# Six small stores from ScalarE in the middle of a decode kernel, and x's load ahead of b1's

## The chip, the core and the metric

The kernel runs on one core of a Trainium2 chip. The core has TensorE (PE in the profile; PEld is its weight load), VectorE (DVE), ScalarE (ACT), GpSimd (POOL) and SyncE (SP), which run side by side and wait for each other by semaphores, and 16 DMA engines that move data between HBM and the on-chip memory. SP and ScalarE each issue DMAs on a queue of their own (q1 and q10 in the profile). The metric is the device time of one execution in microseconds; less is better.

## The reference

One token x of width 1024 goes through a layer norm; the result feeds an attention branch over a cached window and an MLP branch with a layer norm of its own; both are added.

```python
def _A_ref(x, k_cache, v_cache, wq, wo):      # Hq = 32 heads, Hkv = 4, Dh = 128
    W = 4096                                   # the last 4096 of 65536 cached positions
    q = (x @ wq)                               # 1024 -> 32 x 128
    k = jnp.repeat(k_cache[:, :, Sk - W:, :], rep, axis=1)
    v = jnp.repeat(v_cache[:, :, Sk - W:, :], rep, axis=1)
    p = _softmax(scores(q, k) * (Dh ** -0.5))
    return (p @ v).reshape(B, Sq, Hq * Dh) @ wo

def _B_ref(x, w1, b1, w2, b2):                 # F = 3584
    y = _layernorm(x, axis=-1)
    h = _gelu(jnp.einsum("bsd,df->bsf", y, w1) + b1)
    return jnp.einsum("bsf,fd->bsd", h, w2) + b2

xn = _layernorm(A_x, axis=-1)
return A_x + _A_ref(xn, ...) + _B_ref(xn, ...)
```

All inputs and the output are bf16; the output is one row of 1024. The weights and the window of the cache are 39.9 MB, each byte used once.

## The kernel before

The kernel is written out by hand, engine by engine; each engine runs its instructions in the order in which they stand in the code, and `Track` objects count semaphores so that one engine can wait for another's instruction.

*Loads.* SP issues the large loads on one queue, in this order: w1 (L208), K in two halves (L199), wq in two halves (L191, 4 of 8 rows each); then, when PE has finished h (L367), w2 into the place of w1 and V in two halves; then, when PE has finished q (L481), wo in four chunks of 20, 8, 3 and 1 columns (L191) into the place of wq. Each such DMA has one contiguous row for each of 128 partitions: 56 KB for w1 and w2, 32 KB for half of wq, 16 KB for half of K or V, 40 KB for wo's first chunk. ScalarE issues three small loads at the very start: b1's row (L204, 16 pieces of 448 bytes), x's row (L205, 2 KB, one partition) and b2's row (L206).

*Compute.* PE turns x's row into a column (L289), and PE, DVE, POOL and ScalarE do the two layer norms (L292 to L316). PE adds b1 into the PSUM (L350 on; it waits for b1 there) and multiplies by w1 in a loop (h). POOL meanwhile makes constants: identity matrices, masks, zeroed tiles (LB among them, L248). DVE transposes K in eight pieces (turn_k, L326). ScalarE copies h's rows out (L373, L374), PE transposes them, DVE and ScalarE compute the GELU: its exponential is L406 on ScalarE, the only work of ScalarE between L374 and L425. PE multiplies by wq as its halves land (q, paced by SP through `s_row`, L370). After q, ScalarE and DVE copy q's rows (L425, L427); PE transposes them, DVE and ScalarE spread them into LB (L450, L451); PE computes scores against K (L334), DVE their maxima (L480), ScalarE the exponentials (L506), DVE transposes the probabilities (L510). PE then multiplies the MLP's hidden row by w2 (looped by `steps`), the probabilities by V (loop pv, after waiting for both halves of V), and DVE normalizes (L541 to L557). After some extra matmuls that keep PE's clock up (turn_over, L534), PE multiplies by wo as its chunks land: the first two are announced by SP (L562), the last two are waited for by PE. b2 and x are added on PE. ScalarE copies the result to ORow (L579) and stores it as four pieces of 512 bytes from four partitions (L581); SP waits for that store (L582).

L334 is the line of the helper `tile`, by which nearly all of PE's matmuls are issued; L326 is that of `turn_k`, L191 of `load_rows`, L199 of `load_cache`.

Of the kernel before, what the change touches and what calls it, by code (L numbers as in the profile page):

```python
# [10 lines left out]
D = 1024  # L11
# [39 lines left out]
def bass_parallel_sum__sliding_block_cached__mixer_channel_mlp__decode_kernel(  # L51
# [18 lines left out]
    pe, dve, act, pool, sp = nc.tensor, nc.vector, nc.scalar, nc.gpsimd, nc.sync  # L70

    def sems(name, n):
        return [nc.alloc_semaphore(f"{name}{i}") for i in range(n)]

    s_xrow, s_b1, s_b2, s_w1, s_w2, s_out, s_go, s_row = (
        nc.alloc_semaphore(n) for n in ("s_xrow", "s_b1", "s_b2", "s_w1", "s_w2", "s_out", "s_go", "s_row"))
    s_wq = sems("s_wq", len(WQ_CHUNKS))
    s_k = sems("s_k", NPAIR)
    s_v = sems("s_v", NPAIR)
# [5 lines left out]
    POOL = Track(nc, "S_POOL")  # L85

    def sb(name, shape, d):
        return nc.alloc_sbuf_tensor(name, shape, d)
# [14 lines left out]
    XBR = sb("XBR", [1, 2 * D], bf16)  # L103
# [9 lines left out]
    ORow = sb("ORow", [128, 256], bf16)  # L113
    QT = sb("QT", [128, HQ], bf16)
    LB = sb("LB", [128, 8 * 144], bf16)
# [27 lines left out]
    x_row = A_x.rearrange("b s n -> (b s) n")  # L143
# [6 lines left out]
    out_rows = out.rearrange("b s (a n) -> (b s a) n", a=4)  # L150

    C = {}
# [44 lines left out]
    def load_cache(dst, cache, semaphores):  # L197
        for i in range(NPAIR):
# [2 lines left out]
                cache[0, 2 * i:2 * i + 2, SK - W:SK, :].rearrange("g (m b) d -> m g (b d)", m=64),  # L201
            ).then_inc(semaphores[i], 16)

    act.dma_start(B1R, b1_row.rearrange("o (c n) -> o c n", c=B1N)).then_inc(s_b1, 16)  # L204
    act.dma_start(XBR[:, 0:D], x_row).then_inc(s_xrow, 16)  # L205
    act.dma_start(XBR[:, D:2 * D], b2_row).then_inc(s_b2, 16)  # L206

    sp.dma_start(W1[:, :], w1_p).then_inc(s_w1, 16)  # L208
# [14 lines left out]
    def product(out, a, b, ready):  # L223
# [22 lines left out]
    pool.wait_ge(POOL.sem, POOL.cnt)  # L246
    POOL.mark(pool.tensor_tensor(out=BLK[:, :], in0=BLI[:, 0:4], in1=BLI[:, 4:8], op=ALU.add))
    C["lb"] = POOL.mark(pool.memset(LB[:, :], 0.0))  # L248
    POOL.mark(pool.memset(E4[:, :], 0.0))
    POOL.mark(pool.tensor_copy(  # L250
        REP4[:, :].rearrange("p (e q d) -> p e q d", e=4, q=4),
# [4 lines left out]
        out=SAME[:, :].rearrange("p (h b) -> p h b", b=4), in0=HD[:, 0:32].unsqueeze(2).to_broadcast([128, HQ, 4]),  # L256
# [6 lines left out]
    for i in range(NPAIR):  # L263
        C["consts"] = POOL.mark(pool.tensor_tensor(
            out=E4[:, :].rearrange("p (q r) -> p q r", r=129)[:, :, 64 * i:64 * i + 64:4],
# [124 lines left out]
    for i in range(8):  # L390
        n = 128 if i < 4 else 96
# [12 lines left out]
    turn_k(3)  # L404
    act.wait_ge(DVE.sem, C["d_T"])
    C["a_sig"] = ACT.mark(act.activation(out=U2[:, :], in_=U2[:, :], func=ACTF.Exp, scale=-GELU_C))  # L406
    dve.wait_ge(ACT.sem, C["a_sig"])
    DVE.mark(dve.tensor_scalar(out=U2[:, :], in0=U2[:, :], scalar1=1.0, scalar2=None, op0=ALU.add))
    dve.wait_ge(DVE.sem, DVE.cnt)
# [34 lines left out]
    for eng, track, qs in ((dve, DVE, (0, 1)), (act, ACT, (2, 3))):  # L444
        eng.wait_ge(PE.sem, C["rep"])
        eng.wait_ge(POOL.sem, C["lb"])
        for q in qs:
            dst = LB8[32 * q:32 * q + 32, :, 32 * q:32 * q + 16]
            src = PS[32 * q:32 * q + 32, 6 * 512:6 * 512 + 128].rearrange("p (e h) -> p e h", e=8)
# [35 lines left out]
    for a in range(4):  # L485
        for i in range(2):
            src = XBR[0:1, i * D + a * 256:i * D + (a + 1) * 256]
# [17 lines left out]
    for n in range(4):  # L505
        C["exp"] = ACT.mark(act.activation(  # L506
            out=Pb[:, n * 512:(n + 1) * 512], in_=PS[:, n * 512:(n + 1) * 512], func=ACTF.Exp,
# [3 lines left out]
            out=PT.rearrange("p (i c h) -> p c i h", i=NPAIR, h=16)[:, 16 * n:16 * n + 16],  # L511
# [28 lines left out]
    for c in range(1, 4):  # L540
        C["d_od"] = DVE.mark(dve.scalar_tensor_tensor(  # L541
            out=OD[:, :], in0=PS[:, 4 * 512 + 128 * c:4 * 512 + 128 * c + 128], scalar=BLK[:, c:c + 1], in1=OD[:, :],
# [10 lines left out]
    for _ in range(3):  # L553
# [4 lines left out]
        out=OT, in0=PS[:, 6 * 512 + 160:6 * 512 + 192], scalar1=REC[:, 0:1], scalar2=None, op0=ALU.mult))  # L558
# [54 lines left out]
```

## Time and profile before

| | |
|---|---|
| runs (3) | 99.55, 99.68 and 99.71 us; median 99.68 |
| the profiled execution | 99.53 us, of which its span is 98.3 |
| moved over the span | 39.86 MB, mean 406 GB/s |
| busy: PE, PEld, DVE, ACT, POOL | 49.0, 18.4, 31.5, 9.6, 10.1 us |
| mean granted PE clock | 0.844 |

The span runs from the first to the last recorded instruction; the execution's own time is 1.23 us longer. Times in the views count from the span's start. In lists in order of time, the columns are start, duration, engine and line, operation, output and input; what stands in brackets is how long the engine was idle before and which instruction's end released it. A queue's line has packets, MB and the packets' time as a share of the 16 DMA engines over the window; a packet is counted where it starts, so a short window in which long packets start shows more than 100%. In the table of windows, the columns after the stretch are its length, busy time (and instructions) of PE, PEld, DVE, ACT and POOL, the granted PE clock, the DMA share and GB/s. A waits line has the total idle time, how often, and the longest.

### The profile page before, as it was taken

How to read it: one execution, taken by the hardware profiler on the slowest of the kernel's cores; microseconds unless marked ns; L12 is line 12 of the kernel's file. 1: busy time of each engine (PE TensorE's matmuls, PEld its weight loads, DVE VectorE, ACT ScalarE, POOL GpSimd, SP SyncE). 2: the span in 40 equal slices, each digit the busy share in tenths (PEclk: the TensorE clock that was granted, in tenths of full speed). 3: DMA queues.
4: the chain of work that ended last, by engine and by line, in shares of the span. 5: the costliest groups of instructions: out<-in, count | busy, mean ns of one | idle time of the engine just before them, and what ended most of it. 6: DMA issues, size and time to landing. Idle time of an engine off the chain costs nothing.

```text
span 98.3 us, 1233 instructions
## 1 busy us (share of the span) xinstructions
PE 49.0 (50%) x500; PEld 18.4 (19%) x415; DVE 31.5 (32%) x42; ACT 9.6 (10%) x23; POOL 10.1 (10%) x34
## 2 busy tenths in 40 slices
PE   0000022659520700670077589993675599786671
PEld 0000022213110000100010321221433243524240
DVE  0000003270799999993002300415550001300000
ACT  0500000240400000000002200001920001000001
POOL 2000001499940000000000000000000000000000
PEclk9999999999997555559755555999999958999999
DMA  9898888999999999999988889949999979799960
GB/s 350 350 423 373 374 373 374 447 433 427 433 513 440 427 440 440 427 427 427 587 373 373 373 373 513 607 173 427 427 433 513 467 333 533 317 417 427 387 267 1
DMA packets 1773, 39.86 MB, mean 406 GB/s; under 512 B 231, under 2 KB 235, under 8 KB 493
## 3 DMA queue, kind: packets, MB, share of 16 engines
q1 hardware_dynamic: 1728, 39.85, 95.1%
q10 hardware_dynamic: 44, 0.01, 0.1%
q14 instruction: 1, 0.00, 0.0%
HBM read 39.86 MB, written 0.00 MB: 406 GB/s over the span
## 4 chain that ended last, share of the span: by engine, by line
DMA 89%; PE 4%; SPq 4%; issue 1%; ACT 0%
DMA WW<-in_A_wq_dram 47%; DMA WW<-in_A_wo_dram 42%; PE PS L334 4%; SPq L191 2%; SPq L199 1%; ACT ORow L579 0%; SPq L208 0%; SPq L370 0%
## 5 line engine op out<-in xcount | busy, mean ns | idle before, releaser
L326 DVE STREAM_TRANSPOSE KV<-KV 128x2048 bf16<-128x2048 bf16 x8 | 18.5, 2310 | 3.4 <-DMA KV<-in_A_k_cache_dram 3.2
L334 PE MATMUL PS<-WW,XNTb 128*32 x64 | 7.2, 629 | 11.9 <-SPq L370 11.9
L334 PE MATMUL PS<-WW,VEC 128*32 (+1 forms) x240 | 9.5, 275 | 4.9 <-issue 3.2
L334 PE MATMUL PS<-KV,LB 128*128 128x512 bf16 x31 | 9.0, 463 | 1.1 <-DVE LB L450 1.1
L289 PE MATMUL PS<-oneb,XBR 1*128 1x1 bf16 x8 | 0.6, 196 | 13.9 <-DMA XBR<-in_A_x_dram 13.9
L334 PEld LDWEIGHTS PS<-WW,VEC 128*32 (+1 forms) x236 | 5.1, 96 | 9.3 <-issue 9.0
L334 PE MATMUL PS<-KV 128*64 x32 | 5.3, 507 | 1.9 <-DMA KV<-in_A_v_cache_dram 1.9
L334 PE MATMUL PS<-WW,YTb 128*32 x56 | 5.1, 494 | 1.5 <-DMA WW<-in_B_w_dram 1.5
L480 DVE TENSOR_REDUCE MXP<-PS 128x1 f32<-128x1024 f32 x2 | 2.4, 1224 | 8.3 <-PE PS L334 8.3
L292 DVE COPY XT<-PS 128x8 f32<-128x8 f32 x1 | 0.2, 168 | 14.6 <-PE PS L289 14.6
L334 PEld LDWEIGHTS PS<-WW,XNTb 128*32 x32 | 1.2, 114 | 18.4 <-issue 18.4
L541 DVE SCALAR_TENSOR_TENSOR OD<-PS,BLK,OD 128x128 f32<-128x128 f32 x3 | 1.1, 351 | 10.6 <-ACT OD L538 10.5
L334 PE MATMUL PS<-OUTM,PAR 2*128 2x512 bf16 x4 | 1.9, 614 | 4.7 <-DVE HT L397 4.7
L534 PE MATMUL PS<-E,identf 128*128 128x512 f32 x8 | 3.9, 616 | 0.0
L427 DVE CAST Qs<-PS 128x512 bf16<-128x512 f32 x1 | 0.7, 691 | 8.4 <-PE PS L334 8.4
L334 PEld LDWEIGHTS PS<-KV,LB 128*128 128x128 bf16 x16 | 1.9, 117 | 7.7 <-issue 6.9
L510 DVE STREAM_TRANSPOSE KV<-KV 128x512 bf16<-128x512 bf16 x4 | 2.7, 712 | 1.8 <-ACT KV L506 1.8
L334 PEld LDWEIGHTS PS<-KV 128*64 x32 | 2.4, 142 | 4.5 <-issue 4.0
L289 PEld LDWEIGHTS PS<-oneb,XBR 1*128 1x128 bf16 x8 | 0.6, 165 | 13.9 <-issue 13.9
L506 ACT ACTIVATE KV<-PS,BIAS 128x512 bf16<-128x512 f32 x4 | 2.7, 685 | 0.0
L425 ACT ACTIVATE Qs<-PS 128x512 bf16<-128x512 f32 x1 | 0.6, 597 | 20.4 <-PE PS L334 20.4
L334 PEld LDWEIGHTS PS<-WW,YTb 128*32 x32 | 1.5, 107 | 5.4 <-issue 5.2
(93 smaller groups left out, 37.6 us busy)
## 6 DMA issues: line engine op xcount, KB each, us to landing
WW<-in_B_w_dram SPq DMA_DIRECT2D x2, 7168.0 KB, 29.9
WW<-in_A_wq_dram SPq DMA_DIRECT2D x2, 4096.0 KB, 41.7
WW<-in_A_wo_dram SPq DMA_DIRECT2D x1, 5120.0 KB, 35.0
KV<-in_A_k_cache_dram SPq DMA_DIRECT2D x2, 2048.0 KB, 26.0
KV<-in_A_v_cache_dram SPq DMA_DIRECT2D x2, 2048.0 KB, 47.1
WW<-in_A_wo_dram SPq DMA_DIRECT2D x1, 2048.0 KB, 39.5
WW<-in_A_wo_dram SPq DMA_DIRECT2D x1, 768.0 KB, 40.9
WW<-in_A_wo_dram SPq DMA_DIRECT2D x1, 256.0 KB, 41.1
```

The costliest lines, as they stand in the source:

```text
L191: sp.dma_start(dst[:, c0 * width:(c0 + n) * width].rearrange("p (c n) -> p c n", c=n), src[:, c0:c0 + n, :],).then_inc(semaphores[j], 16)
L199: sp.dma_start(dst[:, 2 * i * W:2 * (i + 1) * W], cache[0, 2 * i:2 * i + 2, SK - W:SK, :].rearrange("g (m b) d -> m g (b d)", m=64),).then ...
L289: last = pe.matmul(xt[:, r:r + 1], lhsT=XBR[0:1, r:D:KC], rhs=oneb[0:1, 0:1])
L326: C["kd"] = DVE.mark(dve.transpose(out=KD4[:, n], in_=KR[:, n * 2048:(n + 1) * 2048].rearrange("p (b e s) -> p b e s", b=16, e=4)))
L334: return pe.add_instruction(mybir.InstMatmult(name=nc.get_next_instruction_name(), engine=pe.engine, ins=[lowered(rhs, False), lowered(lhs ...
L425: C["a_qs"] = ACT.mark(act.activation(out=Qs[:, 0:512], in_=PS[:, 6 * 512:7 * 512], func=ACTF.Copy))
L427: C["d_qs"] = DVE.mark(dve.tensor_copy(Qs[:, 512:1024], PS[:, 7 * 512:8 * 512]))
L480: C["mx", half] = DVE.mark(dve.tensor_reduce(out=MXP[:, half:half + 1], in_=PS[:, half * 1024:(half + 1) * 1024], axis=AX.X, op=ALU.max))
L506: C["exp"] = ACT.mark(act.activation(out=Pb[:, n * 512:(n + 1) * 512], in_=PS[:, n * 512:(n + 1) * 512], func=ACTF.Exp, bias=BIAS[:, :], s ...
L510: C["tr", n] = DVE.mark(dve.transpose(out=PT.rearrange("p (i c h) -> p c i h", i=NPAIR, h=16)[:, 16 * n:16 * n + 16], in_=Pb[:, n * 512:(n ...
L534: pe.matmul(PS[:, 3 * 512:4 * 512], lhsT=identf[:, :], rhs=E4[:, 0:512])
L541: C["d_od"] = DVE.mark(dve.scalar_tensor_tensor(out=OD[:, :], in0=PS[:, 4 * 512 + 128 * c:4 * 512 + 128 * c + 128], scalar=BLK[:, c:c + 1] ...
```

## The change

Three edits. x's load is issued ahead of b1's on ScalarE's queue. POOL zeroes ORow, after LB. Right after its exponential for the GELU (L406), ScalarE issues six DMAs that write the result's 1024 values in HBM, and after each it waits until that one has landed, before it goes on: twice four rows of 512 bytes from partitions 0, 32, 64 and 96 of ORow, one row of 2 KB from XBR, two rows of 1 KB from LB, sixteen rows of 128 bytes from ORow, four rows of 512 bytes from partitions 0 to 3 of ORow. What they write is overwritten by the last store.

```diff
+    s_xrow, ..., s_row, s_probe = (...)
...
+    act.dma_start(XBR[:, 0:D], x_row).then_inc(s_xrow, 16)
     act.dma_start(B1R, b1_row.rearrange("o (c n) -> o c n", c=B1N)).then_inc(s_b1, 16)
-    act.dma_start(XBR[:, 0:D], x_row).then_inc(s_xrow, 16)
     act.dma_start(XBR[:, D:2 * D], b2_row).then_inc(s_b2, 16)
...
     C["lb"] = POOL.mark(pool.memset(LB[:, :], 0.0))
+    C["rows0"] = POOL.mark(pool.memset(ORow[:, :], 0.0))
     POOL.mark(pool.memset(E4[:, :], 0.0))
...
     act.wait_ge(DVE.sem, C["d_T"])
     C["a_sig"] = ACT.mark(act.activation(out=U2[:, :], in_=U2[:, :], func=ACTF.Exp, scale=-GELU_C))
+    out_1 = out.rearrange("b s n -> (b s) n")
+    out_2 = out.rearrange("b s (a n) -> (b s a) n", a=2)
+    out_16 = out.rearrange("b s (a n) -> (b s a) n", a=16)
+    act.wait_ge(POOL.sem, C["rows0"])
+    for k, (dst, src) in enumerate((
+            (out_rows, ORow[0:128:32, :]), (out_rows, ORow[0:128:32, :]), (out_1, XBR[0:1, 0:D]),
+            (out_2, LB[0:2, 0:512]), (out_16, ORow[0:16, 0:64]), (out_rows, ORow[0:4, :]))):
+        act.dma_start(dst, src).then_inc(s_probe, 16)
+        act.wait_ge(s_probe, 16 * (k + 1))
     dve.wait_ge(ACT.sem, C["a_sig"])
```

More of the change, by code (lines that the diff above doesn't have):

```diff
@@ L73, in sems @@
         return [nc.alloc_semaphore(f"{name}{i}") for i in range(n)]
-    s_xrow, s_b1, s_b2, s_w1, s_w2, s_out, s_go, s_row = (
-        nc.alloc_semaphore(n) for n in ("s_xrow", "s_b1", "s_b2", "s_w1", "s_w2", "s_out", "s_go", "s_row"))
+    s_xrow, s_b1, s_b2, s_w1, s_w2, s_out, s_go, s_row, s_probe = (
+        nc.alloc_semaphore(n) for n in ("s_xrow", "s_b1", "s_b2", "s_w1", "s_w2", "s_out", "s_go", "s_row", "s_probe"))
     s_wq = sems("s_wq", len(WQ_CHUNKS))
```

## The prediction, made before the changed kernel ran

> **What bounds the kernel now.** I read the chain that ended last first.
>
> ```profile
> DMA 89%; PE 4%; SPq 4%; issue 1%; ACT 0%
> DMA WW<-in_A_wq_dram 47%; DMA WW<-in_A_wo_dram 42%; PE PS L334 4%; SPq L191 2%; SPq L199 1%; ACT ORow L579 0%; SPq L208 0%; SPq L370 0%
> ```
>
> The loads on SP's queue follow each other without a gap from 1.8 to 95.8 us, and the end comes 2.5 us after the last row of wo. So a change costs time only if it lengthens that stream, or if it delays the compute behind it by more than its slack. Next, ScalarE in order of time: its DMA issues (ACTq) and the two instructions around the new code.
>
> ```profile
> 0.81 0.63 ACTq L204 DMA_DIRECT2D KV<-in_B_b_dram  x1
> 1.47 0.89 ACTq L205 DMA_DIRECT2D XBR<-in_A_x_dram  x1
> ...
> 32.78 0.23 ACT L406 ACTIVATE U<-U 128x28 f32<-128x28 f32 x1 [5.73 <-DVE U L403]
> 53.41 0.60 ACT L425 ACTIVATE Qs<-PS 128x512 bf16<-128x512 f32 x1 [20.40 <-PE PS L334]
> ...
> 96.58 0.60 ACTq L581 DMA_DIRECT2D out_dram<-ORow  x1
> ```
>
> The stores have the 20.4 us between L406 and L425. What one costs there is the whole question. The last store, with nothing else moving, was issued at 96.58; its packets moved 0.61 us after its issue ended (97.79), the semaphore stood at 98.2: 1.63 us in all. But in the gap the queues are full. The only small DMAs seen beside a full queue are b1's, x's and b2's loads at the start, so I asked for the DMA packets in short windows. 1.5 to 6.5 us:
>
> ```profile
> q1 hardware_dynamic: 32, 1.84, 97.7%
> ```
>
> 6.5 to 7.2 us:
>
> ```profile
> q1 hardware_dynamic: 16, 0.92, 302.9%
> q10 hardware_dynamic: 16, 0.01, 3.6%
> ```
>
> 8.7 to 9.3 us:
>
> ```profile
> q1 hardware_dynamic: 16, 0.92, 352.8%
> q10 hardware_dynamic: 16, 0.00, 1.5%
> ```
>
> q1 is SP's queue, q10 ScalarE's; each of the 16 DMA engines handles one q1 packet at a time, and a q1 packet is one partition's whole row (w1: 7168 KB / 128 = 56 KB). Each engine starts two rows of w1 before 6.5 us; only then comes its packet of b1's data, then a third row, and at 8.8 to 9.3 us its second small packet, the semaphore. b1 lands 8.8 us after its issue began. x, on one engine behind b1, repeats the pattern: data behind row 4 (11.2 us), semaphore behind row 5 (13.4), landed 13.74. So a small DMA pays two turns, and each turn costs a row of the bulk queue. How long is a row in the gap? The DMA column of the windows counts a packet where it starts (58 to 59: none), so w2's rows show as pulses:
>
> ```profile
> 57.00:58.00 1.00, 1.00 (x3) 0.23 (x2) 0.00 (x0) 0.00 (x0) 0.00 (x0) 0.50 1.99 860
> 58.00:59.00 1.00, 1.00 (x3) 0.15 (x1) 0.00 (x0) 0.00 (x0) 0.00 (x0) 0.50 0.00 0
> 59.00:60.00 1.00, 1.00 (x4) 0.15 (x1) 0.00 (x0) 0.00 (x0) 0.00 (x0) 0.50 2.12 918
> 60.00:61.00 1.00, 1.00 (x4) 0.15 (x1) 0.00 (x0) 0.00 (x0) 0.00 (x0) 0.50 0.00 0
> ```
>
> The second half of wq (32 KB rows, eight per engine) lands between 39.8 and 49.44 us: 1.21 us a row. w2 (56 KB rows) follows until 66.4: 2.12 us a row. Last, the slack behind L425, from the waits of PE:
>
> ```profile
> PE PS L334 <- DMA KV<-in_A_v_cache_dram: 1.9, 1, 1.9
> PE PS L334 <- SPq L562: 1.6, 2, 0.9
> PE PS L334 <- DMA WW<-in_B_w_dram: 1.5, 1, 1.5
> ```
>
> **The change, part by part.**
>
> *x ahead of b1.* x's packet now takes the place behind row 2 of its engine and lands near 9.4 us instead of 13.74; b1's share on that engine moves to 13.75, b2 stays at 18. The layernorm chain ends some 4.3 us earlier (y at 15.4 instead of 19.75). Then PE waits for w1, which lands at 20.2 and already costs it the 1.5 us above: h, w2's issue behind it and K's transposes stay where they are. PE reaches b1's seven matmuls (1.0 us) by 14, so they too fit ahead of w1. Gain and cost: zero, covered by the wait for w1.
>
> *A memset of ORow on GpSimd.* 128x256 bf16, between L248's 128x1152 (1.06 us) and identb's 128x128 (0.20 us): 0.2 to 0.3 us on an engine that is done at 28.2 us, and that now starts 4.3 us earlier. Zero; the store's wait for it is long satisfied at 33 us.
>
> *Six stores.* Each is issued, then ScalarE waits for its semaphore, and behind that wait stand L425 and all later work of ScalarE. Issue: 0.60 (L581), other rows 0.21 to 0.89; I take 0.6. To the engine: 0.61. Then, as b1 did, it finds a row running, lets the next row pass too, puts its data down, waits one more row for the semaphore packet, and lands 0.35 us later (x: 13.40 to 13.74). Rows start within 0.5 us of each other on the 16 engines; the times below are the latest engine that a store uses (4, 4, 1, 2, 16 and 4 engines, one per row of its shape).
>
> - 1: from 32.9; at the engine 34.1; running row ends 35.1, next 36.4, data; semaphore 37.6; landed 38.0.
> - 2: at the engine 39.3; rows end 40.5 and 41.7; semaphore 42.9; 43.2.
> - 3: at the engine 44.5; 45.3 and 46.5; 47.7; 48.1.
> - 4: at the engine 49.4, now among w2's rows; 51.1 and 53.2; 55.2; 55.6.
> - 5: at the engine 56.9; 57.4 and 59.5; 61.6; 62.0.
> - 6: at the engine 63.3; 63.7 and 65.9; w2 ends there, and v follows with its short rows; 66.2.
>
> The stores last 33.3 us where 20.4 are free. ScalarE takes L425 at 66.3 instead of 53.41: **12.9 us late**. The bytes are nothing: q10's 0.1% of 16 engines over 44 packets is 36 ns a packet, twelve on the busiest engine 0.4 us, which counts only if the stream still sets the end.
>
> Why not another price? With one row less (strict turns) the six land at 36, 39.5, 43.2, 46.8, 49 and 53.5, and ScalarE is free at 53.6, or at 55.5 if each arrives 0.3 us later; with one row more at 70.3. With issues of 0.21 us it is 62.1; with 0.89, 66.9. I take one row let past, as on all 16 engines of b1. That is a load at the start of the stream; a store into a running stream is shown nowhere, and this is the weakest step. Still, b1's issue ended at 1.44, so it should be at the engines about 2.05, long before the first row ended (4.5 to 5.0); the second went ahead all the same.
>
> The Trainium skill, "DMA: Bandwidth & Descriptors" (Anatomy of one DMA), speaks against this: it gives every DMA a constant cost of about 2.0 us, nearly all of it waiting for the write's receipt, with nothing in it for another queue. Six would be about 12 us (an estimate from that page), hidden in the gap. The idle store's 1.63 us bears that out; b1's 8.8 us does not.
>
> *Where the 12.9 us go.* Minus 0.1: the cast on VectorE (L427, 0.69) had set the pace, not L425 (0.60). Minus 0.9: v landed at 76.2 and PE idled 1.9 us for it, of which 1.0 is the loop's own set-up after the landing. Minus 1.1: the two waits for wo (0.86 and 0.79, where steps without one are 0.25 apart) vanish, since all of wo has landed. Minus 1.7: the half clock from 78.4 to 81.8 followed the idle stretch before the v product; without it those 3.4 us of work take half as long. The scores, half their time at half clock before, start cold again at about 69.3: no change, give or take 1.2 us. Nothing else is late: wo's issue (L481) waits for q alone. Sum: 12.9 - 0.1 - 0.9 - 1.1 - 1.7 = 9.1. On the profiled execution's 99.53 us that is 108.6; the median of the runs lies 0.15 above that execution, so **108.7 us**.
>
> Break-even: about 2 us late (0.9 + 1.1), 3.7 with the clock's share, so a store may last (20.4 + 2 to 3.7) / 6 = 3.7 to 4.0 us.
>
> **The rivals.**
> - *Strict turns* (not slower): a new packet goes ahead right after the running row. ScalarE is free at 53.6 to 55.5, the lateness falls into the 2 to 3.7 us of slack, the stream sets the end: 99.5 to 100.0 us, by the extra packets. For it: x's and b2's packets do alternate with single rows once they queue. Against it: b1's first. Chance 0.08.
> - *The idle price* (not slower): 6 x 1.63 = 9.8 us, over at 42.7; 99.5 to 100.0. For it the last store, against it b1 and x. Chance 0.04.
> - *Dearer stores*: more rows let past, or the write receipts into a busy memory, or 128-byte pieces over 16 engines: free at 70 to 74, 112.6 to 116.5 us. For it: nothing was seen of stores in a busy stream. Chance 0.08.
> - *x pays*: only if h had waited for y; y was ready at 19.75, w1 at 20.2, and the stream would hold the end in any case. At most 0.3 us faster. Chance 0.01. That x lands no earlier would cost nothing.
>
> **How the numbers follow.** My case (62.1 to 70.3, so 104.4 to 112.6) has 0.79, and its likeliest point is 108.7. The range is that case's, widened by the scores' clock on the far side: 104.3 to 113.0. It leaves out the two hidden cases and most of the dear one, under 0.2 together. A measurement of this kernel can tell 0.2% (0.2 us) from no change; the hidden cases fall on both sides of that through the extra packets. Faster 0.02, same 0.06, slower 0.92.
>
> **What would show it.** Six pairs of ACTq issues and waits from 32.9 us on, 4 to 5 us apart while wq loads and 6 to 7.5 among w2's rows; L425 near 66 us, released by a store; no wait for v and none for wo; XBR's wait of PE 9.5 instead of 13.9; the chain at the end through PE and ACT instead of wo's DMA. Stores 3.5 us apart and L425 still at 53 to 55 would show the forecast wrong.

## The result and the profile after

The changed kernel takes 112.87 us (111.87 to 113.09) against 99.69: a ratio of 1.1315 with a 95% interval of 1.1271 to 1.1358. Forecast: 108.7, range 104.3 to 113.0. A ratio counts only runs within 1.5% of the fastest run of their kernel, a median all of them; of the ten runs with four stores below, which spread over 3.2%, the ratio counts the five shortest. The profiled execution took 113.09 us with a span of 111.7.

The page's chain that ended last, by engine and by line (the last entries of the second line are small):

```profile
DMA 56%; PE 27%; DVE 10%; issue 3%; ACT 2%; SPq 0%; DVEq 0%; ACTq 0%
DMA out_dram<-ORow 22%; DMA KV<-in_A_k_cache_dram 21%; PE PS L335 21%; DMA out_dram<-XBR 7%; DVE KV L327 6%; DMA out_dram<-LB 6%; PE PS L544 2%; DVE MXP L490 1%; DVE OD L551 1%; PE PS L560 1%; PE PS L441 1%; ACT Qs L435 1%; DVE LB L460 1%; DVE MXH L505 0%; ACT ORow L589 0%
```

The bulk loads of wq and wo are gone from it (before, they made 89% of it). In their place stand the stores (out_dram) and then compute, PE above all. The same chain in order of time, start and duration, around the stores:

```profile
32.81 6.51 DMA out_dram<-ORow
39.34 6.55 DMA out_dram<-ORow
45.91 7.94 DMA out_dram<-XBR
53.87 6.37 DMA out_dram<-LB
60.26 6.35 DMA out_dram<-ORow
66.63 4.90 DMA out_dram<-ORow
71.61 0.60 ACT Qs L435
```

Six stores, one behind the other, 38.6 us. Each duration is issue, wait and landing together. ScalarE's copy of q (L435, formerly L425) starts at 71.61 instead of 53.41. The waits say the same from the other side, with PE idle behind ScalarE:

```profile
ACT Qs L435 <- DMA out_dram<-ORow: 38.6, 1, 38.6
PE PS L441 <- ACT Qs L435: 18.9, 1, 18.9
PE PS L290 <- DMA XBR<-in_A_x_dram: 2.3, 1, 2.3
```

The third line is x's load: PE gets x after 2.3 us instead of 13.9.

What does a store wait for? The first one's issue ended at 33.40. The DMA queues from 33.4 to 36.6 us:

```profile
q1 hardware_dynamic: 40, 1.31, 94.8%
```

Then 36.6 to 37.7 us, and 37.8 to 38.9 us:

```profile
q1 hardware_dynamic: 13, 0.43, 89.8%
q10 hardware_dynamic: 4, 0.00, 0.6%
```

```profile
q1 hardware_dynamic: 16, 0.39, 83.1%
q10 hardware_dynamic: 4, 0.00, 0.2%
```

For 3.2 us nothing of ScalarE's queue (q10) moves, while 40 rows of wq begin, 2.5 for each of the 16 engines. Then come its four data packets, and one wq row (1.2 us) later its four semaphore packets. The last store, in the idle queue, waits 0.65 us between the end of its issue (110.57) and its data.

### The profile page after: what moved, and what is told of

It reads as the page before. It is cut to its first block, busy times and chain, and to the rows that moved or that the text cites. A ratio compares the mean times of both kernels' runs of the same rounds, so it can differ in the third digit from the quotient of the medians.

```text
span 111.7 us, 1242 instructions
## 1 busy us (share of the span) xinstructions
PE 49.7 (44%) x501; PEld 18.6 (17%) x415; DVE 31.5 (28%) x42; ACT 9.6 (9%) x23; POOL 10.4 (9%) x35
## 4 chain that ended last, share of the span: by engine, by line
DMA 56%; PE 27%; DVE 10%; issue 3%; ACT 2%; SPq 0%; DVEq 0%; ACTq 0%
DMA out_dram<-ORow 22%; DMA KV<-in_A_k_cache_dram 21%; PE PS L335 21%; DMA out_dram<-XBR 7%; DVE KV L327 6%; DMA out_dram<-LB 6%; PE PS L544 2%; DVE MXP L490 1%; DVE OD L551 1%; PE PS L560 1%; PE PS L441 1%; ACT Qs L435 1%; DVE LB L460 1%; DVE MXH L505 0%; ACT ORow L589 0%
## 5 line engine op out<-in xcount | busy, mean ns | idle before, releaser
L335 PE MATMUL PS<-WW,VEC 128*32 (+1 forms) x240 | 10.1, 306 | 2.4 <-issue 2.2
L335 PE MATMUL PS<-WW,YTb 128*32 x56 | 6.2, 574 | 10.1 <-DMA WW<-in_B_w_dram 10.1
L335 PE MATMUL PS<-KV,LB 128*128 128x512 bf16 x32 | 10.0, 486 | 0.7 <-DVE LB L460 0.7
L441 PE MATMUL PS<-identb,Qs 128*128 128x128 bf16 x8 | 1.0, 305 | 18.9 <-ACT Qs L435 18.9
L335 PEld LDWEIGHTS PS<-WW,VEC 128*32 (+1 forms) x236 | 5.6, 104 | 7.0 <-issue 6.6
L441 PEld LDWEIGHTS PS<-identb,Qs 128*128 128x128 bf16 x8 | 0.8, 136 | 20.2 <-issue 20.2
L435 ACT ACTIVATE Qs<-PS 128x512 bf16<-128x512 f32 x1 | 0.6, 597 | 38.6 <-DMA out_dram<-ORow 38.6
L335 PE MATMUL PS<-KV 128*64 x32 | 3.6, 380 | 0.4 <-issue 0.4
L335 PE MATMUL PS<-KV,oneb 1*32 1x512 bf16 x7 | 1.0, 612 | 3.0 <-DMA KV<-in_B_b_dram 3.0
```

What stands on the lines that cost most here:

```text
L335: return pe.add_instruction(mybir.InstMatmult(name=nc.get_next_instruction_name(), engine=pe.engine, ins=[lowered(rhs, False), lowered(lhs ...
L435: C["a_qs"] = ACT.mark(act.activation(out=Qs[:, 0:512], in_=PS[:, 6 * 512:7 * 512], func=ACTF.Copy))
L441: last = pe.matmul(PSb[:, 7 * 1024 + 128 * i: 7 * 1024 + 128 * (i + 1)], lhsT=Qs[:, i * 128:(i + 1) * 128], rhs=identb[:, :], is_transpose ...
```

## The experiments

All times are medians; the kernel before, on the same chip, is 99.50 to 99.67 us. The theory: the whole cost is ScalarE's wait for its turn at the DMA engines, and the work queued behind that wait. First the parts of the change.

**x's load alone** (no stores)

```diff
+    act.dma_start(XBR[:, 0:D], x_row).then_inc(s_xrow, 16)
     act.dma_start(B1R, ...).then_inc(s_b1, 16)
-    act.dma_start(XBR[:, 0:D], x_row).then_inc(s_xrow, 16)
```

> Only x's load ahead of b1's, no stores. Theory (the whole cost is ScalarE's waits): x lands near 2.1 us as in the changed kernel, h ends up to 1 us later on a cold PE, the loads still set the end: 99.6 to 99.9 us. Rival (the earlier layer norm pays or the colder h costs): under 99.4 or over 100.2 us.

99.55 us, ratio 0.9993 (0.9981 to 1.0004). PE has x 11.4 us earlier (after a wait of 2.5 us instead of 13.9), and it buys nothing. One part of the expectation failed: h was to end up to 1 us later, and ScalarE's copy of it starts at 25.88, where it started at 25.98 before.

**The stores alone** (the old order of the loads)

```diff
+    act.dma_start(B1R, ...).then_inc(s_b1, 16)
     act.dma_start(XBR[:, 0:D], x_row).then_inc(s_xrow, 16)
-    act.dma_start(B1R, ...).then_inc(s_b1, 16)
```

> The six stores, loads in the old order. Theory: the same six waits, L435 at 71 to 72 us, 112.4 to 113.2 us. Rival (x's move has a share in the 13 us): more than 1 us below.

112.78 us, ratio 1.1322 (1.1294 to 1.1349): all of the loss. L435 starts at 71.42.

**Three stores, four stores**

```diff
-            (out_2, LB[0:2, 0:512]), (out_16, ORow[0:16, 0:64]), (out_rows, ORow[0:4, :]))):
+            )):                                    # three
+            (out_2, LB[0:2, 0:512]))):             # four
```

> Only the first three stores (4, 4 and 1 rows). Theory: they end at 53.8 us as in the changed kernel, ScalarE takes its next work at 53.9, 0.5 us late, inside the slack of V's wait: 99.6 to 100.1 us. Rival (each store costs its sixth of 13.2 us, 2.2): 106.3 us.

> The first four stores. Theory: the fourth ends at 60.2 us, ScalarE is 6.9 us late; the slack that the changed kernel used up was 18.2 - 13.5 = 4.7 us, so 2.2 us stay: 101.9 us (101 to 103). Rival (2.2 us each): 108.5 us.

Three: 99.59 us, ratio 0.9998 (0.9985 to 1.0012). ScalarE's timeline:

```profile
46.74 0.23 ACTq L415 DMA_DIRECT2D out_dram<-XBR  x1
53.69 0.60 ACT L435 ACTIVATE Qs<-PS 128x512 bf16<-128x512 f32 x1 [20.45 <-PE PS L335]
```

The copy of q waits for PE, not for a store: the third landed just before. Four: a median of 101.37 us over ten runs, which spread from 99.83 to 103.05; the ratio, 1.0071 (1.0044 to 1.0098), is lower than the medians make it. A likely reason for the spread is that a store's wait depends on where in a row it arrives, but only one of the ten runs has a trace, so this is not shown. In its profiled execution (101.26 us) L435 starts at 60.22. So the cost is not a sixth per store: the first three are free, the fourth costs about 2 us, the last two 11.5 between them.

**Smaller stores, with and without the wait**

```diff
...
+    out_32 = out.rearrange("b s (a n) -> (b s a) n", a=32)
+    for k in range(6):
+        act.dma_start(out_32[4 * k:4 * k + 4, :], ORow[0:4, 0:32]).then_inc(s_probe, 16)
+        act.wait_ge(s_probe, 16 * (k + 1))        # with
...
     act.wait_ge(PE.sem, C["fin"])
+    act.wait_ge(s_probe, 96)                      # without: once, ahead of the last copy
```

> Six stores of four pieces of 64 bytes to six disjoint parts of the result, each waited for. Theory (a store waits for the queue, not for its bytes): about 6.4 us each as before, ScalarE free at 70 to 73 us, 111.5 to 114 us. Rival (bytes count): the 2 KB stores were 8 to 32 times larger, so these take under 4 us each and hide, 99.7 us.

> The same six stores of 64-byte pieces, without a wait between them; one wait for all of them ahead of the last store. Theory (the cost is the wait that ScalarE's next work stands behind): six issues of 0.2 to 0.6 us, 99.6 to 100.2 us. Rival (the packets themselves disturb the loads): 103 us and more.

With waits 109.55 us (108.88 to 111.54), ratio 1.0983 (1.0942 to 1.1025): below the 111.5 that I expected. The only trace is of the longest run, 111.54 us, where the copy of q (L434 there) starts at 71.44, as expected; why the other three were 1.8 to 2.7 us shorter no trace shows. But an eighth of the bytes still costs 10 us. Without waits 99.58, ratio 1.0007 (0.9989 to 1.0025). Its queues from 35.5 to 50 us:

```profile
q1 hardware_dynamic: 210, 6.23, 99.7%
q10 hardware_dynamic: 48, 0.00, 0.2%
```

All 24 data and 24 semaphore packets take their turns there, and the loads lose nothing by it. The first four move at 36.5 us, 3.3 us after the end of the first issue; then every engine that is used takes one packet of the stores after each row, some 1.2 us apart, and the last semaphore packets move at 48.7. So stores that queue behind each other pay the long lead once and are all done by about 49 us, where six that are waited for one by one need until 71.

**Loads in place of the stores**

```diff
...
+            (ORow[0:128:32, :], x_4), (ORow[0:128:32, :], x_4), (XBR[:, D:2 * D], b2_row),
+            (ORow[0:2, :], x_4[0:2, :]), (ORow[0:16, 0:64], x_16), (ORow[0:4, :], x_4))):
```

> Loads in place of the six stores, each waited for, with nearly the shapes of the stores (4, 4, 1, 2, 16, 4 rows; the two rows are 512 bytes instead of 1 KB): x's row into ORow, b2's row once more into XBR. Theory (what is waited for is the turn on each DMA engine, whichever way the bytes go): 6 to 8 us each as for the stores, ScalarE free at 70 to 73 us, 111.5 to 114 us. Rival (a store's receipt from HBM under load is the dear part): loads take 4 to 5 us, free at 57 to 63 us, 100 to 104 us.

112.49 us, ratio 1.1301 (1.1263 to 1.1338). Its chain:

```profile
32.79 6.59 DMA ORow<-in_A_x_dram
39.40 7.31 DMA ORow<-in_A_x_dram
46.73 6.98 DMA XBR<-in_B_b_dram
53.73 7.99 DMA ORow<-in_A_x_dram
61.74 5.46 DMA ORow<-in_A_x_dram
67.22 4.92 DMA ORow<-in_A_x_dram
```

Loads wait as long as stores, so the receipt of a write to HBM is not the dear part.

**GpSimd issues and waits**

```diff
...
-        act.dma_start(dst, src).then_inc(s_probe, 16)
-        act.wait_ge(s_probe, 16 * (k + 1))
+        pool.dma_start(dst, src).then_inc(s_probe, 16)
+        pool.wait_ge(s_probe, 16 * (k + 1))
...
+    act.wait_ge(s_probe, 96)                      # ahead of the last copy
```

> The same six stores and waits, issued by GpSimd after the exponential instead of by ScalarE (the two rows come from Hs instead of LB); ScalarE waits for them only ahead of its last copy. Theory: GpSimd has nothing else to do after 28 us, so its waits hold up nobody: 99.6 to 100.3 us, with stores of 6 us and more. Rival (stores in this stretch slow the loads or PE): over 102 us.

99.67 us, ratio 1.0012 (0.9993 to 1.0032). GpSimd's timeline:

```profile
40.07 0.58 POOL L415 DMA_DIRECT2D out_dram<-ORow  x1 [5.97 <-DMA out_dram<-ORow]
47.30 0.49 POOL L415 DMA_DIRECT2D out_dram<-XBR  x1 [6.64 <-DMA out_dram<-ORow]
56.01 0.53 POOL L415 DMA_DIRECT2D out_dram<-Hs  x1 [8.22 <-DMA out_dram<-XBR]
```

It waits as long or longer (6.0, 6.6 and 8.2 us behind the issue), and nobody stands behind it. The packets are not quite the same: GpSimd's queue (q0 in its trace) moves the 2 KB row as 32 packets, ScalarE's as one of data and one for the semaphore.

**Shorter rows in the stream.** The prediction counted rows. To see whether rows are what passes ahead of a store, each half of wq is loaded by several DMAs of shorter rows (`cols` 2048 or 256):

```diff
-    load_rows(WA, wq_p, WQ_CHUNKS, NQ, s_wq)
+    for j in range(2):
+        for c in range(0, NQ, cols):
+            sp.dma_start(WA[:, j * 4 * NQ:(j + 1) * 4 * NQ].rearrange(...)[:, :, c:c + cols],
+                         wq_p[:, 4 * j:4 * j + 4, c:c + cols]).then_inc(s_wq[j], 16)
...
```

> The changed kernel with each half of wq loaded by two DMAs of 4 KB rows (four per partition) instead of one of 32 KB rows; stores 1 to 3 begin among them. In the trace of the changed kernel and the runs after it the first data packet of a store follows the end of its issue by at least 3.1 us, whether rows are 16, 32 or 56 KB, against 0.6 in the idle queue. Theory (a fixed lead of some 2.5 us or 64 KB per engine, then a turn of one row): data 3.1 to 3.4 us after the issue's end, semaphore a 0.15 us row later, store 1 and 2 about 4.3 us each instead of 6.5. Rival of the prediction (whole rows are counted, one or two let past): data within 1.1 us, each store about 2.2 us.

> As the run with 4 KB rows, but 512-byte rows, which move at a lower rate (27 to 33 ns per 512 bytes in the last store, 16 to 19 GB/s against 27). If the lead is a time: data 3.1 us after the issue's end again. If it is 64 KB per engine: 128 rows of 28 ns, 3.6 us, so data about 4.2 us after. If a number of rows: under 1 us. The loads themselves take some 10 us longer.

With 4 KB rows (108.25 us, one run) the first store's issue ended at 33.83. The queues from 33.84 to 37.1 us, then 37.1 to 37.5:

```profile
q1 hardware_dynamic: 352, 1.38, 102.7%
```

```profile
q1 hardware_dynamic: 41, 0.17, 101.9%
q10 hardware_dynamic: 8, 0.00, 2.2%
```

21 rows per engine begin ahead of the store, not two or three (1.38 MB over 16 engines and 4 KB rows; the other 16 of the 352 packets are semaphores of the loads); then data and semaphores together, a short row apart. Store 1 lasts 4.7 us and store 2 5.5, where 32 KB rows had made each 6.5. The expectation was 4.3: store 2's data came 3.9 us and more after its issue, and why is open. PE finished q at 55.9 us instead of 53.4, so the shorter rows slowed wq's own load. With 512-byte rows the issue ended at 33.42, and from there to 36.1, and from 36.1 to 36.5:

```profile
q1 hardware_dynamic: 1567, 0.78, 116.9%
```

```profile
q1 hardware_dynamic: 234, 0.11, 115.0%
q10 hardware_dynamic: 8, 0.00, 2.5%
```

The first store's data came 2.7 to 3.0 us after the issue, behind 95 rows of 512 bytes per engine, or 49 KB (0.78 MB over 16 engines); the first four stores last 4.5 us each. That is nearer to a fixed time than to the 4.2 us that 64 KB per engine would have made. But SP's issue itself runs slowly here (wq's issues last until 54 us), so less may have been queued ahead; whether the lead is a time or a number of bytes stays open. The run's 109.0 us are no price of the stores: L439 (the copy of q there) was released by PE at 63.2, because wq came in later.

**One engine or sixteen**

```diff
+    for k in range(6):
+        act.dma_start(out_16, ORow[0:16, 0:64])...   # or out_1, XBR[0:1, 0:D]
```

> Six times the store of sixteen 128-byte rows, on 16 engines. Theory: each waits for the unluckiest of 16 engines, data up to 3.1 us plus a whole row after the issue; among 32 KB rows 0.6 + 4.3 + 1.2 + 0.4 = 6.5 us, among 56 KB rows up to 0.3 + 5.2 + 2.1 + 0.4 = 8.0 us: three before 53 us, all six over at 73 to 78 us, 113 to 118 us. Rival (small pieces cost a read and rewrite): over 9 us each.

> Six times the store of one 2 KB row, on one engine. Theory: one engine draws a wait between the least and the most, 5 to 6.5 us among 32 KB rows and 5.8 to 8 us among 56 KB rows: all six over at 66 to 73 us, 107 to 114 us; never longer than the sixteen-engine stores. Rival (one engine must move all bytes, so it is slower): later than the sixteen-engine stores.

Sixteen pieces of 128 bytes: 114.72 us, one row of 2 KB: 107.56 (one run each). The chain of the first:

```profile
32.95 6.52 DMA out_dram<-ORow
39.49 6.51 DMA out_dram<-ORow
46.03 7.87 DMA out_dram<-ORow
53.92 8.22 DMA out_dram<-ORow
```

and of the second:

```profile
32.93 5.48 DMA out_dram<-XBR
38.43 6.14 DMA out_dram<-XBR
44.59 5.13 DMA out_dram<-XBR
49.74 6.20 DMA out_dram<-XBR
```

The same 2 KB are stored sooner in one piece: a store waits for the last of the engines that it uses. In the first store the sixteen data packets moved between 3.1 and 4.5 us after the end of the issue, the single packet after 3.5. Sixteen pieces also take longer to issue, 0.32 to 0.38 us against 0.21 to 0.23, which makes 0.8 us of the 6.6 that lie between the two copies of q (73.58 and 67.00).

## Where the prediction was right and where it was wrong

*Right: what decides.* The stores are priced by the queue, ScalarE's later work stands behind their waits, the slack takes some of it, and the rest goes into the end. Strict turns and the idle price fall: the shortest of these stores in any run took 4.3 us, above the break-even of 3.7 to 4.0. The Trainium skill's constant of about 2.0 us per DMA ("DMA: Bandwidth & Descriptors", Anatomy of one DMA, a section on DMAs that GpSimd issues) is near the idle store from ScalarE (1.6 us) and far below all of these (4.3 to 8.5 us from ScalarE, 5.7 to 8.7 from GpSimd).

*Wrong in size: the step "a row running, lets the next row pass too".* It made the stores 33.3 us and L425 start at 66.3; they took 38.6, and the copy of q started at 71.6. In every run with rows of 16, 32 or 56 KB a store's data follows the issue by at least 3.0 us, and by up to about a row more (5.6 at most); the idle queue shows 0.6. So a store arriving in a stream meets at least about 2.4 us of work that goes ahead, plus the rest of a row. What makes this lead, a time or a number of bytes, and where it is spent, no run settles. With w1's 56 KB rows at the start that looked like "one more row". Among wq's 32 KB rows two or more went ahead of each store: stores 1 to 3 took 6.5, 6.6 and 7.9 us, not the forecast's 5.1, 5.2 and 4.9. Store 3 waited so long that w2's rows reached it: its data moved at 51.2 us, and its semaphore packet paid a row of w2 (2.2 us). Among w2's rows, like those it was read from, the step was nearly right: stores 4 and 5 took 6.4 and 6.4, forecast 7.5 and 6.4. The prediction named this as its weakest step. The second turn, a row for the semaphore packet, held for stores 1 to 4 (1.2 us among wq's rows, 2.2 among w2's), and so did 0.35 to 0.45 us to land.

*Inside the range by luck.* The median lies 0.13 us below the range's upper end, and the profiled execution, 113.09 us, above it. The copy of q at 71.6 is later than the 70.3 that the prediction's own case allowed; it belongs to the rival of dearer stores (free at 70 to 74, 112.6 to 116.5 us), which had a chance of 0.08. With 18.2 us of lateness in place of 12.9 the prediction's own sum (less 0.1, 0.9, 1.1 and 1.7) gives 14.4 and 114.1 us, outside the range. A second error, the waits for v and wo taken 1.5 us too small, brought the time back.

*The sum, term by term*, from the two profiled executions:

| term | forecast | measured | from |
|---|---|---|---|
| L425/L435 later | +12.9 | +18.2 | 53.41, 71.61 |
| cast on VectorE | -0.1 | 0.0 | PE's transposes 54.16, 72.36 |
| scores' clock | 0 (1.2 either way) | +0.5 | last maximum +18.7 (66.00, 84.73) |
| wait for v | -0.9 | -1.5 | rows' sum 74.93, 93.66; v product 77.21, 94.40 |
| half clock in the v product | -1.7 | -1.7 | L538/L548 82.58, 98.09 |
| waits for wo | -1.1 | -2.0 | L557/L567 85.36, 100.86; L579/L589 96.17, 109.64 |
| sum | +9.1 | +13.5 | |

The execution as a whole became 113.09 - 99.53 = 13.6 us longer. The clock's term is shown by PE's timeline, before and after: the v product takes 3.64 us instead of 5.33, and starts at once.

```profile
77.21 5.33 PE L334 MATMUL PS<-KV 128*64 x32 [1.90 <-DMA KV<-in_A_v_cache_dram]
...
88.84 0.62 PE L334 MATMUL PS<-WW,VEC 128*32 x16 [0.86 <-SPq L562]
```

```profile
93.66 0.38 PE L527 MATMUL PS<-SUMP,SAME 128*128 128x1 f32 x2
94.40 3.64 PE L335 MATMUL PS<-KV 128*64 x32 [0.36 <-issue]
...
103.41 0.62 PE L335 MATMUL PS<-WW,VEC 128*32 x16
```

The two waits were worth more than I took: the loop's set-up, put down as 1.0 us after v's landing, leaves only 0.36 us of idle when nothing is waited for, and wo's first step now follows the extra matmuls at once. The 4.7 us between +18.2 and +13.5 are the slack that the fourth store used up.

*Right by its cover, wrong in its number: x.* It was to land at 9.4 us behind row 2 of w1 and landed at 2.15: issued first, its packet started 0.38 us after its issue ended (at 1.72 us) and was ahead of the first row of w1 on any engine (1.80). It still buys nothing, as the wait for w1 covers it. Beside that, h ran at 574 ns a matmul instead of 494 and ended 1.1 us later (ScalarE's copy of it at 27.09 instead of 25.98). That was not forecast; it too is covered, as w2's load stands behind wq's rows. PE's longer idle stretch ahead of h does not explain it. Before, after, and x's load alone, in this order:

```profile
20.81 5.12 PE L334 MATMUL PS<-WW,YTb 128*32 x56 [1.52 <-DMA WW<-in_B_w_dram]
20.85 6.20 PE L335 MATMUL PS<-WW,YTb 128*32 x56 [10.15 <-DMA WW<-in_B_w_dram]
20.88 4.96 PE L334 MATMUL PS<-WW,YTb 128*32 x56 [10.06 <-DMA WW<-in_B_w_dram]
```

After the same idle stretch h is as fast with x's load alone as before, and the granted clock reads 1.00 in all three; the cause stays open.

## What to carry to other kernels

A small DMA in a stream of bulk loads is priced by the stream: here its issue, some 3 us, up to one row of the bulk DMA, one row more for its semaphore, and 0.4 us to land, 4.3 to 8.5 us for 2 KB or less where the idle queue takes 1.6. Idle time of an engine is free for such DMAs only as long as all the waits end before its next instruction is due; count that wait times the number of DMAs, against the gap plus the slack behind it. If the data are not needed there, issue without waiting and wait once late, or let an engine wait that nobody stands behind; DMAs that queue behind each other pay the lead once. Fewer and larger pieces shorten the wait itself. So do shorter rows in the bulk loads, but here they made wq late: q ended 2.5 us later with 4 KB rows and 9.8 us later with 512-byte rows.

## What was not expected of the hardware

- At least about 2.4 us of the stream's work goes ahead of a small DMA that reaches busy DMA engines (data 3.0 us or more after the issue's end, 0.6 when idle), whether rows are 4, 16, 32 or 56 KB; with 512-byte rows it was at least 2.1 (2.7 after the issue).
- Loads and stores of nearly the same shapes wait alike from ScalarE, 4.9 to 8.0 and 4.9 to 7.9 us; GpSimd's stores, from issue to issue, took 5.7 to 8.7.
- 48 small packets among the bulk rows left no trace in the time (ratio 1.0007), though each of them took a turn.
